# Block 1: another order of weight groups, its second item in f16 halves, and the weights' scales ahead of its first item

## The chip, the cores and the metric

The kernel runs on one core of one Trainium2 chip. The metric is device microseconds of one execution; lower is better. The time before is the median of three runs.

## What is computed

Linear attention with two softmaxes gives a matrix x of 4608 tokens by 512; a two-layer network with an unusual activation follows it.

```python
def _attn_ref(q, k, v):                       # each (8, 8, 576, 64), f32
    q_s = softmax(q, axis=-1)                 # written out: max, exp, sum + 1e-9
    k_s = softmax(k, axis=2)
    kv = np.einsum('bhsd,bhse->bhde', k_s, v)
    return np.einsum('bhsd,bhde->bhse', q_s, kv)

def _moe_ref(x, w_in, w_out):                 # (4608, 512), (512, 2048), (2048, 512)
    h = x @ w_in
    sp = np.maximum(h, 0.0) + np.log1p(np.exp(-np.abs(h)))
    g = h * erf(sp)
    return g @ w_out
```

w_in and w_out arrive as 64-bit floats, two 32-bit words to a number, and the kernel decodes them to f32 itself.

## The kernel before

**Items.** The tokens are cut into 4 pairs of batches, a pair (1152 tokens) into 3 blocks of 384, and the hidden width of 2048 into 4 groups of 512. One block with one group is an *item*; there are 48, numbered n in the order of `seq` (L942). Item n has a first product `m{n}` (x of the block by w_in of the group, in four parts m{n}.0 to m{n}.3), then on ScalarE softplus `T{n}` and erf `G{n}`, on VectorE the product with h `U{n}`, and a second product `M{n}` with w_out of the group, in three parts by 128 tokens, added up in PSUM over the block's four items. T and G each load a table on ScalarE.

**Two forms.** Items below `N32` = 6 run in f32: `mm1_32` (L1027) is 16 matmuls of 128x384, with four ScalarE copies out of PSUM, and `mm2` has 12 matmuls of 128x512. Items from 6 on run in f16 halves, high and low, of both operands with three products for one: `mm1` (L974) is seven block products in a scheme with fewer multiplications (84 matmuls of 128x192, evacuated by three ScalarE copies and four VectorE operations), and `mm2` has 36 matmuls of 128x512. For such an item VectorE also makes the high half `I{n}` (a cast, L1092) and the low half `O{n}` (a subtraction, L1096) of the activated values.

**What the f16 form needs.** Each weight half-matrix (a *job* j of `JOBS`: in 0, in 1, out 0, in 2, out 1, in 3, out 2, out 3) is loaded, decoded (`D`, VectorE) and squared for its maximum (`Q`, ScalarE). When all eight are squared, `Z` (`wscales`, L254) reduces the maxima, turns them on TensorE (8 transposes into the banks pY and pZ), and computes scales and the units U and V on VectorE. Then `S{j}` (`wsplit`, L306) writes the high halves on ScalarE and the low halves on VectorE (`split2`, L299 to L301) and, for a w_in, also four sums in place (L327); `R{j}` splits the sums. S{j} writes where the staged f32 of job j-2 lay. `f` (`finish`, L374) does the same for the block's x: an even f splits the parts as they are, an odd f the differences, in place in the f32 x that `mm1_32` of the block reads.

**Order.** `ORDER` (L33) is written out by hand up to item 5. Behind it a loop (L1225) emits, for n from N32 on, U{n-1}, the parts of m{n} with I{n-1}, O{n-1} and M{n-2} between them, then the splits that `SPLITS` (L46) names for n, then T{n} and G{n}. The attention of batches 1 to 7 is a generator: a token `A` in ORDER takes one step of it, and in the loop `pace` (L1208) takes steps as items go by. Batch 1 has 17 steps; the first step of a batch is the maximum over k on VectorE (L518 to L522), the second its transposes kT on TensorE with the reduction km (L529, L533) and the subtraction of q's maximum for the first four heads (L465, L466). ORDER takes 19 steps. Exponentials of a batch from 2 on, softplus and erf keep their written order on ScalarE.

The framework then schedules all engines' instructions, with the written order as priority: an instruction that is ready may run ahead of one that is not, so that the trace shows some steps earlier than the text has them. At run time each engine's own order is fixed.

Of the kernel before, what the change touches and what calls it, by code (L numbers as in the profile page):

```python
# [35 lines left out]
    m0.0 m0.1 D0.0.1 D0.1.1 D1.0 D1.1 m0.2 m0.3 T0 G0 Q0  # L36
    D2.0 A m1.0 D2.1 m1.1 U0 m1.2 m1.3 T1 G1 Q1 A A D3.0 M0.0 D3.1 M0.1 M0.2 Q2 U1 A A
    m2.0 D4.0 m2.1 D4.1 m2.2 m2.3 T2 G2 Q3 A A D5.0 M1.0 D5.1 M1.1 M1.2 U2 A A Q4 D6.0
    m3.0 D6.1 m3.1 D7.0 m3.2 D7.1 m3.3 T3 G3 A A A A A A A A A A Q5 U3 Q6 Q7
    M2.0 M2.1 M2.2 m4.0 m4.1 Z m4.2 m4.3 T4 G4 M3.0 f0 M3.1 M3.2 S0 R0 m5.0 m5.1 U4 m5.2 m5.3  # L40
    T5 G5 f1 S1 R1
"""


N32 = 6
SPLITS = {6: "S2 S4", 7: "S6 f2 f3 S3 R3", 8: "S5 R5", 9: "S7"}  # L46

SHARES = [2.51, 0, 0.16, 0.09, 1.58, 2.43, 1.12, 0.26, 0.29, 0.04, 0.78, 1.12, 0.16]
LEAD = 2.0
# [7 lines left out]
def attn_moe_kernel(  # L57
# [14 lines left out]
    NP = B // 2  # L72
# [6 lines left out]
    NG = NF // FG  # L79
# [3 lines left out]
    NBK = PT // T  # L83
# [260 lines left out]
    def act(out_, in_, func, chain=True, **kw):  # L344

        with ExitStack() as es:
            if chain and last[0] is not None:
                es.enter_context(tc.issue_after(last[0]))
            i = nc.scalar.activation(out_, in_, func, **kw)  # L349
        if chain:  # L350
            last[0] = i.ins
        return i
# [19 lines left out]
    x_next = [1]  # L372
# [555 lines left out]
    def out_dmas(p, tt, src):  # L928
# [11 lines left out]


    seq = [  # L942
        (p, bk, (g + 2 * (p == 0 and bk == 1)) % NG)
        for p in range(NP) for bk in range(NBK) for g in range(NG)
    ]
    N = len(seq)
# [96 lines left out]
    def unit(b, g):  # L1043

        U = bat[b]["U"][:, g:g + 1]
        if b < 2 and (b, g) not in udone:
            udone.add((b, g))
            nc.vector.tensor_tensor(U, w_u["in"][:, g:g + 1], bat[b]["ux"], op=ALU.mult)
        return U
# [3 lines left out]
    def flat(t):  # L1053
        return t.rearrange("p f t -> p (f t)")

    def in_chain(n):
        return CHAIN_FROM <= n < N - CHAIN_TAIL

    def softplus(n):
        s, g = st[n], seq[n][2]  # L1060
        s["G"] = ch.tile([P, FG, T], F32, tag="G", bufs=2, name=f"G_{n}")
        for o, w, b in spans(n):
            h, sp = s["H"], s["G"]
            h, sp = (flat(t) if w == T else t[:, :, o:o + w] for t in (h, sp))
            u = 1.0 if n < NG else bat[b]["ux"] if n < N32 else unit(b, g)
            act(sp, h, AF.Softplus, chain=in_chain(n), scale=u)
# [5 lines left out]
    def gmul(n):  # L1072
        s, g = st[n], seq[n][2]
        if n < NG:
# [3 lines left out]
        nc.vector.scalar_tensor_tensor(  # L1078
            flat(s["G"]), flat(s["G"]), GA32 if n < N32 else GA[:, g:g + 1], flat(s["H"]),
            op0=ALU.mult, op1=ALU.mult,  # L1080
        )
        if n < N32:
            return
# [18 lines left out]
    def mm2(n, tt):  # L1102
# [8 lines left out]
        ts_ = slice(tt * P, (tt + 1) * P)  # L1111
        if n < N32:
            w = stg[jn].rearrange("p (a e) -> p a e", a=FG)
# [37 lines left out]
    def tok(name):  # L1151

        if name != "A":
            if name in done:
                return
            done.add(name)
        if name in steps:
            dep, f = steps[name]
            assert all(x in emitted_steps for x in dep.split()), name
            f()  # L1160
            emitted_steps.add(name)
            if all(f"y{c}" in emitted_steps for c in range(NC4)):
                bat[0]["xdone"] = True
            return
        c = name[0]
        if c == "A":
            r = next(att, None)
            share[0] += r or 0
            return r
        x = [int(i) for i in name[1:].split(".")] if name[1:] else []  # L1170
        if c == "w":
            warm(*x)
        elif c == "D":
            with tc.issue_after(decoded[0].ins) if x[2:] == [1] else ExitStack():
                wdecode(NPC * x[0] + x[1], *x[2:])
        elif c == "Q":
            wsquares(*x)
        elif c == "S":
            wsplit(*x)
        elif c == "R":  # L1180
            wsplit_sums(*x)
        elif c == "f":
            xready(x_next[0])
            finish(x[0] % 2)
        elif c == "Z":
            wscales()
        elif c == "m":
            (mm1_32 if x[0] < N32 else mm1)(*x)
            emitted.add(("m", *x))
        elif c == "M":  # L1190
            mm2(*x)
            emitted.add(("M", *x))
        else:
            fn[c](*x)
# [13 lines left out]
    def pace(at_n):  # L1208


        at_n += LEAD
        k = NBK * NG + NG
        if at_n < k:
            goal = w_odd + (at_n - n1) * per_pair / (k - n1)
        else:
            goal = w_odd + per_pair + (at_n - k) * per_pair / (NBK * NG)
        while share[0] < goal:
            if not tok("A"):
                break
# [4 lines left out]
    FIN = 2  # L1224
    for n in range(N32, N + 2):  # L1225
        m0, m1, m2 = n < N, n - 1 < N, n - 2 < N
        if m1:
            tok(f"U{n - 1}")
        for i in range(4):
            if m0:  # L1230
                tok(f"m{n}.{i}")
            if N32 < n <= N and i < 2:
                tok(f"{'IO'[i]}{n - 1}")
            if m0 and n % NG == FIN and n > N32 and i < 2 and x_next[0] < NP * NBK:
                tok(f"f{fi[0]}")
                fi[0] += 1
            if m2 and i < 3:
                tok(f"M{n - 2}.{i}")
                pace(n + (i + 1) / NTT)
        for o in SPLITS.get(n, "").split():  # L1240
            tok(o)
        if m0:
            tok(f"T{n}")
            tok(f"G{n}")
# [32 lines left out]
```

## Time and profile before

| | |
|---|---|
| median of 3 runs | 839.77 us (837.84 to 843.3) |
| the profiled execution | 839.42 us, span 837.6 us |
| TensorE busy | 811.6 us, 97% |
| VectorE busy | 624.0 us, 74% |
| ScalarE busy | 503.9 us, 60% |

The span is the time from the first to the last instruction of the profiled execution; the device time lies 1.8 us above it. TensorE's matmuls are pipelined: the time of one is read from start to start of neighbours, and a row's duration is longer than that. In the timelines a group of like instructions is one row, with its count, and the idle time of the engine in front of it in brackets, with what ended it.

### The profile page before, as it was taken

How to read it: one execution, taken by the hardware profiler on the slowest of the kernel's cores; microseconds unless marked ns; L12 is line 12 of the kernel's file. 1: busy time of each engine (PE TensorE's matmuls, PEld its weight loads, DVE VectorE, ACT ScalarE, POOL GpSimd, SP SyncE). 2: the span in 40 equal slices, each digit the busy share in tenths (PEclk: the TensorE clock that was granted, in tenths of full speed). 3: DMA queues.
4: the chain of work that ended last, by engine and by line, in shares of the span. 5: the costliest groups of instructions: out<-in, count | busy, mean ns of one | idle time of the engine just before them, and what ended most of it. 6: DMA issues, size and time to landing. Idle time of an engine off the chain costs nothing.

```text
span 837.6 us, 15532 instructions
## 1 busy us (share of the span) xinstructions
PE 811.6 (97%) x6546; PEld 547.3 (65%) x6546; DVE 624.0 (74%) x887; ACT 503.9 (60%) x645; POOL 15.9 (2%) x37
## 2 busy tenths in 40 slices
PE   5999999999999999999999999999999999999996
PEld 4555455676666667767676676766776766767762
DVE  6999889998898779767875779857875657554543
ACT  2797759876665746645754556555764565544432
POOL 2101000000000000000000000000000000000000
PEclk9999999999999999999999999999999999999999
DMA  9995710041127205311362204411130100100100
GB/s 259 408 223 183 185 44 38 1 108 39 51 55 154 77 1 105 91 27 27 84 125 51 64 2 93 104 26 27 54 62 14 39 1 1 39 1 1 39 1 38
DMA packets 141348, 61.55 MB, mean 73 GB/s; under 512 B 130528, under 2 KB 132576, under 8 KB 141280
## 3 DMA queue, kind: packets, MB, share of 16 engines
q1 hardware_dynamic: 139104, 52.18, 25.1%
q0 software_dynamic: 2176, 8.39, 2.8%
q8 instruction: 51, 0.84, 0.4%
q14 instruction: 17, 0.14, 0.1%
HBM read 45.09 MB, written 9.44 MB: 65 GB/s over the span
## 4 chain that ended last, share of the span: by engine, by line
PE 59%; DVE 19%; ACT 13%; DMA 4%; issue 3%; SPq 2%; ACTq 0%; DVEq 0%
PE o L1124 25%; PE pX L998 14%; PE pZ L998 6%; ACT G L349 4%; ACT L349 4%; PE pY L998 3%; DVE G L1078 3%; DVE H L1096 2%; PE o L1115 2%; SPq L420 2%; DMA q<-in_q_dram 2%; PE pX L1037 2%; PE kv L565 1%; DVE x L301 1%; PE x L680 1%
## 5 line engine op out<-in xcount | busy, mean ns | idle before, releaser
L1124 PE MATMUL o<-wt,H 128*128 128x512 f16 x1512 | 347.3, 379 | 1.7 <-DVE H L1092 1.3
L998 PEld LDWEIGHTS <-wt 128*128 128x128 f16 x3528 | 293.1, 98 | 37.3 <-issue 15.8
L1124 PEld LDWEIGHTS <-H 128*128 128x128 f16 x1512 | 145.9, 98 | 150.9 <-DVE H L1092 1.8
L998 PE MATMUL pX<-x,wt 128*128 128x192 f16 x2016 | 194.3, 246 | 6.2 <-DVE H L1020 3.3
L349 ACT ACT_TABLE_LOAD x104 | 133.4, 1283 | 8.7 <-DVE H L1023 6.9
L1078 DVE SCALAR_TENSOR_TENSOR G<-G,small,H 128x1536 f32<-128x1536 f32 x44 | 80.0, 1818 | 55.3 <-ACT G L349 55.2
L1025 ACT COPY H<-pX 128x384 f32<-128x384 f32 x42 | 19.9, 474 | 139.2 <-PE pX L998 139.2
L998 PE MATMUL pZ<-x,wt 128*128 128x192 f16 x1008 | 98.4, 246 | 0.0
L349 ACT ACTIVATE G<-H,U 128x768 f32<-128x768 f32 (+1 forms) x56 | 69.2, 1253 | 22.1 <-DVE H L1023 21.5
L1096 DVE TENSOR_TENSOR H<-G,H 128x1536 f16<-128x1536 f32 x42 | 73.7, 1755 | 0.8
L349 ACT ACTIVATE G<-G 128x1536 f32<-128x1536 f32 x48 | 71.2, 1484 | 0.5
L998 PE MATMUL pY<-x,wt 128*128 128x192 f16 x504 | 48.4, 246 | 0.0
L454 ACT ACTIVATE x<-x 128x384 f32<-128x384 f32 (+1 forms) x52 | 16.2, 397 | 48.0 <-PE x L680 48.0
L1023 DVE TENSOR_TENSOR H<-pZ,H 128x384 f32<-128x384 f32 x42 | 23.2, 552 | 26.3 <-PE pZ L998 26.2
L1010 DVE COPY H<-pY 128x384 f32<-128x384 f32 x42 | 23.2, 553 | 26.1 <-PE pY L998 26.0
L300 ACT ACTIVATE x<-x 128x768 f16<-128x768 f32 (+1 forms) x44 | 33.0, 764 | 15.4 <-DVE x L393 15.4
L1092 DVE CAST H<-G 128x1536 f16<-128x1536 f32 x42 | 40.2, 957 | 0.8
L301 DVE SCALAR_TENSOR_TENSOR x<-x,x 128x768 f16<-128x768 f32 (+1 forms) x44 | 37.3, 851 | 3.2 <-ACT x L300 3.2
L1140 DVE TENSOR_SCALAR ob<-o,V 128x512 f32<-128x512 f32 x29 | 21.7, 747 | 21.1 <-PE o L1124 21.1
L1037 PE MATMUL pX<-x,wt 128*128 128x384 f32 x96 | 34.0, 488 | 0.0
L1012 DVE TENSOR_TENSOR H<-pX,H 128x384 f32<-128x384 f32 x42 | 23.3, 555 | 13.7 <-PE pX L998 12.9
L465 DVE TENSOR_REDUCE q_m<-q 128x16 f32<-128x1024 f32 x14 | 17.0, 1216 | 18.0 <-DMA q<-in_q_dram 18.0
(183 smaller groups left out, 818.8 us busy)
## 6 DMA issues: line engine op xcount, KB each, us to landing
out_dram<-ob SPq DMA_DIRECT2D x32, 256.0 KB, 2.3
vbuf<-in_v_dram SPq DMA_DIRECT2D x56, 128.0 KB, 3.2
q<-in_q_dram SPq DMA_DIRECT2D x56, 128.0 KB, 3.2
k<-in_k_dram SPq DMA_DIRECT2D x56, 128.0 KB, 3.2
wt<-in_moe_w_out_dram POOLq DMA_DIRECT2D x5, 1024.0 KB, 6.5
wt<-in_moe_w_in_dram SPq DMA_DIRECT2D x4, 1024.0 KB, 12.0
wt<-in_moe_w_out_dram SPq DMA_DIRECT2D x2, 1024.0 KB, 15.7
H_raw<-in_k_dram SPq DMA_DIRECT2D x2, 512.0 KB, 4.6
```

The lines of the kernel that those rows point to most:

```text
L300: nc.scalar.activation(hi, src, AF.Copy, scale=s)
L301: nc.vector.scalar_tensor_tensor(lo, src, s, hi, op0=ALU.mult, op1=ALU.subtract)
L349: i = nc.scalar.activation(out_, in_, func, **kw)
L998: nc.tensor.matmul(o, w[wl][:, c, a * P:(a + 1) * P], x[:, xl, xi, c, :], start=(new and a == 0 and c == 0 and i == 0), stop=(c == 1 and i ...
L1010: nc.vector.tensor_copy(C[0, 0], bank2("Y"))
L1012: add(C[0, 0], bank2("X"), C[0, 0], op=ALU.add)
L1023: add(C[0, 1], bank2("Z"), C[0, 1], op=ALU.add)
L1037: nc.tensor.matmul(ph[:, :T], w[:, c, a * P:(a + 1) * P], x[:, c, :], start=(c == 0), stop=(c == NC4 - 1),)
L1078: nc.vector.scalar_tensor_tensor(flat(s["G"]), flat(s["G"]), GA32 if n < N32 else GA[:, g:g + 1], flat(s["H"]), op0=ALU.mult, op1=ALU.mult,)
L1092: nc.vector.tensor_copy(flat(s["gh"]), flat(s["G"]))
L1096: nc.vector.tensor_tensor(flat(s["gl"]), flat(s["G"]), flat(s["gh"]), op=ALU.subtract)
L1124: nc.tensor.matmul(o, s[gt][:, a, ts_], w[wl][:, a, :], start=(first_ and a == 0 and i == 0), stop=(last_ and a == FG - 1 and i == 2),)
```

## The change

Three things. Block 1's four items take the groups in the order 3 0 1 2 instead of 2 3 0 1, so that item 4 has group 3 and items 5, 6, 7 have groups 0, 1, 2. `N32` becomes 5: item 5, the second of block 1, runs in f16 halves. And in the order written by hand Z stands in front of m4, two attention steps fewer are taken (17, which is batch 1; the other two, the first of batch 2, are left to `pace`), f1 comes directly behind S0 and R0, and the splits from S1 on move into the loop, where they follow one another in the order in which items 6 to 11 need them. The last edit keeps the loop's own `f` steps where they were (from n = 10 on), now that N32 is smaller.

```diff
-    m3.0 D6.1 m3.1 D7.0 m3.2 D7.1 m3.3 T3 G3 A A A A A A A A A A Q5 U3 Q6 Q7
-    M2.0 M2.1 M2.2 m4.0 m4.1 Z m4.2 m4.3 T4 G4 M3.0 f0 M3.1 M3.2 S0 R0 m5.0 m5.1 U4 m5.2 m5.3
-    T5 G5 f1 S1 R1
+    m3.0 D6.1 m3.1 D7.0 m3.2 D7.1 m3.3 T3 G3 A A A A A A A A Q5 U3 Q6 Q7
+    M2.0 M2.1 M2.2 Z m4.0 m4.1 m4.2 m4.3 T4 G4 M3.0 f0 M3.1 M3.2 S0 R0 f1
 """
 
 
-N32 = 6
-SPLITS = {6: "S2 S4", 7: "S6 f2 f3 S3 R3", 8: "S5 R5", 9: "S7"}
+N32 = 5
+SPLITS = {4: "", 5: "S1 R1 S2", 6: "S3 R3 S4", 7: "S6 f2 f3", 8: "S5 R5", 9: "S7"}
@@
     seq = [
-        (p, bk, (g + 2 * (p == 0 and bk == 1)) % NG)
+        (p, bk, (g + 3 * (p == 0 and bk == 1)) % NG)
         for p in range(NP) for bk in range(NBK) for g in range(NG)
     ]
@@
-            if m0 and n % NG == FIN and n > N32 and i < 2 and x_next[0] < NP * NBK:
+            if m0 and n % NG == FIN and n > 2 * NG and i < 2 and x_next[0] < NP * NBK:
                 tok(f"f{fi[0]}")
                 fi[0] += 1
```

## Rows read from the trace of the kernel before

**Rows 1.** The page: busy time of each engine, then tenths in 40 slices.

```profile
PE 811.6 (97%) x6546; PEld 547.3 (65%) x6546; DVE 624.0 (74%) x887; ACT 503.9 (60%) x645; POOL 15.9 (2%) x37
...
PE   5999999999999999999999999999999999999996
...
DVE  6999889998898779767875779857875657554543
```

**Rows 2.** Busy time by stretch: us, engines' busy us (count), clock, DMA.

```profile
110.14:217.60 107.46, 104.37 (x683) 66.52 (x682) 98.17 (x157) 77.14 (x95) 0.63 (x2) 1.00 0.19 49
217.60:837.60 620.00, 607.76 (x5343) 424.91 (x5341) 429.90 (x594) 351.03 (x414) 2.52 (x8) 1.00 0.20 47
```

**Rows 3.** TensorE's timeline, m4 to m9: start us, us, line, out<-in, count, [idle before].

```profile
110.14 2.74 PE L1037 MATMUL pX<-x,wt 128*128 128x384 f32 x8
113.50 0.63 PE L529 MATMUL kT<-ident,asc 128*128 128x128 f32 x4 [0.62 <-DVE asc L522]
...
116.55 0.60 PE L264 MATMUL ws_out<-ident,small 128*128 128x128 f32 x4
...
122.59 10.46 PE L1115 MATMUL o<-rw,G 128*128 128x512 f32 x24
132.89 2.74 PE L1037 MATMUL pX<-x,wt 128*128 128x384 f32 x8
...
143.21 1.15 PE L998 MATMUL pY<-x,wt 128*128 128x192 f16 x12
...
149.35 1.07 PE L998 MATMUL pX<-x,wt 128*128 128x192 f16 x11 [0.45 <-DVE x L301]
...
182.61 1.15 PE L998 MATMUL pY<-x,wt 128*128 128x192 f16 x12
...
184.59 2.75 PE L1124 MATMUL o<-wt,H 128*128 128x512 f16 x12
187.18 0.27 PE L125 MATMUL x_bk<-ident,mx 128*128 128x128 f32 x1
...
198.37 1.15 PE L998 MATMUL pX<-x,wt 128*128 128x192 f16 x12 [0.91 <-DVE H L1020]
```

**Rows 4.** Groups by line over the span: busy us, mean ns | idle before.

```profile
L998 PEld LDWEIGHTS <-wt 128*128 128x128 f16 x3528 | 293.1, 98 | 37.3 <-issue 15.8
```

**Rows 5.** VectorE's timeline, from the maxima's reduction to f3's last piece.

```profile
108.63 0.18 DVE L258 TENSOR_REDUCE small<-sq 128x8 f32<-128x32 f32 x1
...
113.28 1.20 DVE L465 TENSOR_REDUCE q_m<-q 128x16 f32<-128x1024 f32 x1
...
118.27 0.69 DVE L268 TENSOR_REDUCE wse_in<-ws_in 128x4 f32<-128x512 f32 x1 [2.06 <-PE ws_in L264]
...
122.04 3.14 DVE L301 SCALAR_TENSOR_TENSOR wt<-wt,small,wt 128x1024 f16<-128x1024 f32 x3
...
126.36 3.69 DVE L327 TENSOR_TENSOR wt<-wt 128x512 f32<-128x512 f32 x6
...
132.48 4.87 DVE L301 SCALAR_TENSOR_TENSOR wt<-wt,small,wt 128x1024 f16<-128x1024 f32 x4
...
165.43 1.27 DVE L301 SCALAR_TENSOR_TENSOR wt<-wt,small,wt 128x1024 f16<-128x1024 f32 x1
...
176.78 0.95 DVE L1092 CAST H<-G 128x1536 f16<-128x1536 f32 x1
177.65 0.55 DVE L1020 TENSOR_TENSOR H<-pX,H 128x384 f32<-128x384 f32 x1
178.11 1.75 DVE L1096 TENSOR_TENSOR H<-G,H 128x1536 f16<-128x1536 f32 x1
179.78 0.95 DVE L301 SCALAR_TENSOR_TENSOR x<-x,x 128x768 f16<-128x768 f32 x1
```

**Rows 6.** ScalarE's timeline: T4 from its table load, G4's erf.

```profile
124.39 1.28 ACT L349 ACT_TABLE_LOAD   x1
...
129.22 1.48 ACT L349 ACTIVATE G<-G 128x1536 f32<-128x1536 f32 x1
```

## Prediction

> **What bounds the kernel now.** I read the busy line and the slices first [rows 1]: TensorE is busy 811.6 of 837.6 us, and after the first of the 40 slices it falls below nine tenths only in the last. VectorE is at 74% over the span, but unevenly: its digits are 8 and 9 in the first third and 5 to 7 later. So I cut the span at the end of item 2's second product (110.14) and at the end of item 9's first part (217.60), the stretch that the change touches [rows 2]. The granted clock is 1.00 in both parts. In the first TensorE is busy 104.37 of 107.46 us, VectorE 98.17, ScalarE 77.14. From 217.60 to the end VectorE is busy 429.90 of 620.00. The reader is to see two things: a microsecond of TensorE work that goes away shortens the program if nothing makes TensorE wait in its place, and in just this stretch VectorE has only 9 us left over.
>
> The profiled execution took 839.42 us (span 837.6), which is 0.35 below the median of 839.77. All sums are made against 839.42. About 1%, 8.4 us, is what a measurement of this kernel can tell from no change.
>
> **The change part by part.**
>
> *Item 5 on TensorE.* In f32 its first product is four tiles, from 132.89 to 143.21: 10.32 us. An f32 second product runs from 122.59 to 132.89: 10.30 us [rows 3]. In f16 halves the first product is seven groups of 12 matmuls, two of which took 1.98 (182.61 to 184.59), so 6.93 us; the second is three groups of 2.59 (184.59 to 187.18), so 7.77 us. Item 5 therefore gives back 3.39 + 2.53 = 5.92 us of TensorE. The new order of groups (item 4 is group 3, items 5, 6, 7 are groups 0, 1, 2) costs nothing by itself: same shapes, same count.
>
> Against that stands a rule. The f16 halves need 120 weight loads for item 5 where f32 needs 56 records. A load of f16 weights has a mean of 98 ns [rows 4], and yet the pitch of the 192-column matmuls is 0.99/12 = 82 ns [rows 3]: less than one load, so loads must run under matmuls and under each other. The Trainium skill, "TensorE: Matmul & The Clock Gate", Part 3 (The mechanism), says that a weight load overlaps with matmuls in flight only where the row group differs; here all 128 rows are used each time, so by that rule every load would stand in series. This trace contradicts it, so I keep 14.70 us for the f16 item.
>
> *Scales (Z) in front of m4.* Today the transposes start inside m4, at 116.55 [rows 3], although the maxima they turn were there from the reduction at 108.63 [rows 5]. VectorE idles 2.06 us for the second set of them, and the first split starts at 122.04: 5.49 us after 116.55. In front of m4 they run at 110.14, so splits can start at 110.14 + 5.49 = 115.6, which is 6.4 earlier. The transposes are the same eight, so TensorE pays nothing more; m4 waits for nothing of Z but for the bank of m4.1, which is read within 2 us while m4.0 runs 2.58. Should the reduction be late, nothing covers TensorE: it has 1.3 us to spare (110.14 against 108.63 and its 0.2).
>
> *The two steps of batch 2's attention later.* The k maximum, its transposes (kT) and the first q subtraction lose their early place. TensorE waited 0.62 us in front of kT at 113.50 [rows 3]; that wait goes, kT itself moves behind M4. On VectorE, the second q subtraction and km, which ran from 113.28 to 116.21 (2.06 before 118.27) [rows 5], no longer fit in front of Z's answers: 2.93 us go behind them. The first q subtraction and the k maximum can still run in the gap around 107 to 113, since instructions that are ready run ahead of their place here: S5 of item 8's turn ran at 165.43 [rows 5]. No DMA is moved by these two steps, on SP or POOL; loads of batch 3 hang on later steps.
>
> *Item 5 on VectorE and ScalarE.* VectorE gains the cast (0.87, 176.78 to 177.65), the low half (1.67, 178.11 to 179.78) and four evacuations of 0.47 each (177.65 to 178.11), 4.4 us in all [rows 5]. ScalarE loses one of four copies, at nothing.
>
> *The splits earlier.* All of them still run, none twice. What changes is when they are due. S0, R0 and f1 are due at m5 instead of m6, and f1 must wait for m4 to have read the block, until the eight transposes (some 0.9, the four of kT took no more than 0.63) and m4's 10.3 have run from 110.14 on, so to 121.4. M3 covers TensorE from there to 131.7. VectorE needs for S0 4.3 us (low halves of 1.22 and 0.62, four sums of 0.61), for R0 two of 1.22 and for f1 3.6 (four subtractions of the size of an evacuation, 0.47, two halves of 0.87), 10.3 in all [rows 5]: from 115.6 to 125.9. So m5 does not wait by this sum, with 5.8 us to spare. After that S1, R1, S2, S3, R3 follow one item ahead of their old place.
>
> *Where it gets tight.* I follow VectorE to the last piece of f3, which m8.1 needs. Today it ends at 179.78 + 0.87 = 180.65 [rows 5], and m8 starts at 182.61 [rows 3]. After the change: 180.65 + 4.4 (item 5) + 2.9 (moved behind Z) - 6.4 (Z earlier) - 2.5 (S5's two low halves and one sum, 1.22, 0.62 and 0.61, which ran early as filling and are not due) = 179.1. TensorE would reach m8 at 182.61 - 5.92 - 0.62 = 176.1, or at 175.6 if the short wait on the way (0.45 at 149.35 [rows 3]) vanishes as well. So VectorE, which was 2 us ahead of TensorE at this point, will be behind it: by 3.5 at most, or by 1.5 if m8.0, which runs 1.98 and needs only f2, goes first. M6 could cover it altogether if its halves are ready. The bounds are 0 and 3.5 here, and again up to 0.9 at m9, where TensorE already waits for VectorE (198.37 [rows 3]). I take 2.0 for both together, nearer to the wait of 0.45 at 149.35, where M4 filled in, than to a full stop.
>
> *Sum:* -5.92 - 0.62 + 2.0 = -4.5 us, all of it in hand by about 217; behind that TensorE's work is the same and VectorE is at 69%. 839.42 - 4.5 = 834.9 us.
>
> **The rivals.**
>
> 1. *Nothing gets short.* M6 covers f3, and the waits at 149.35 and 198.37 vanish: -5.92 - 0.62 - 0.45 - 0.91 = -7.9, so 831.5. For it: M4 covered the late f1 at 149.35 but for 0.45. Against it: M5 is 2.53 shorter as a cover, and ScalarE's k and q exponentials stand in front of item 6's softplus.
>
> 2. *VectorE sets the pace through item 9.* Everything that it does up to 199 stays due; then TensorE is where VectorE lets it be: today's wait at 198.37, plus 4.4 + 2.9 - 6.4 = +0.9. The gain is gone but for what it wins back later: 837 to 840. For it: 98.17 busy of 107.46 [rows 2]. Against it: S5, R5 and S7, about 9 us, are not due until m11 and M11.
>
> 3. *Slower: m5 waits at its head.* Place: the high halves of f1 on ScalarE. T4 and G4 are issued ahead of them, and took from 124.39 to 130.70 today [rows 6]. If, in addition, VectorE takes S1 and R1 (6.7) first, f1 ends not at 125.9 but at 125.9 + 6.7 + 6.3 = 138.9, and m5.1, due at 133.7, waits 5.2; M4 cannot fill in, as it needs U4, which stands behind G4. It decides from a wait of 4.5 us on (5.92 + 0.62 less the 2.0 at m8 and m9); at 5.2 the time is 840.1, and if U4 and the copies of M3's output get in front too, some 4 us more, 844. Against it: f1's subtractions can run from 121.4, ahead of T4's end.
>
> 4. *Loads in series.* This is a mechanism by rows: if each of item 5's 120 f16 matmuls paid its load of 98 ns on top of its pitch, the item would cost 14.70 + 11.8 = 26.5 us instead of 20.6, and the program 839.42 + 5.9 - 0.6 = 844.7. The pitch of 82 ns excludes it. (This is the rule of the Trainium skill named above, "TensorE: Matmul & The Clock Gate", Part 3.)
>
> **How the numbers follow.** Forecast (a gain of 2.5 to 6, so 833.4 to 837): 0.56. Rival 1 (830.5 to 833.4): 0.21. Rival 2 (837 to 840.5): 0.14. Rival 3 (839.9 to 850): 0.08. Rival 4: 0.01. Predicted is 834.9. The range leaves out the lower edge of rival 1 (0.06) and most of rival 3 (0.06 with rival 4): 831.0 to 841.0. Faster by over 1% means below 831.4, which is more than all the TensorE work and the waits counted: only the edge of rival 1, 0.08. Slower by over 1% means over 848.2: the far part of rival 3, several such delays behind one another, 0.03. Within 1%: 0.89.
>
> **What would show it right or wrong.** In the changed profile: m5 in f16 shapes starts right behind M3, near 131.7, with no wait over 1 us (rival 3 falls, or shows here). The ws transposes stand ahead of m4 near 110 and the first split of weights starts on VectorE near 115.6. TensorE's records fall by one item's f32 groups, its busy time by 5.9. Item 8's first matmul starts between 175 and 179; a wait there names VectorE's x halves (L301) if my tight place is right, ScalarE's copies if the exponentials are. Item 10, at 217.60 today, starts 4 to 6 earlier, and from there the two traces run side by side. I am wrong if a wait of over 3 us appears on TensorE between 110 and 217, or if that lead is lost later.

## The result, and the profile after

The changed kernel took 831.78 us (median of 5 runs, 831.66 to 833.22), 0.9916 of the kernel before [0.9895, 0.9936]: 7.1 us less by the ratio (the medians lie 8.0 apart; the ratio is used throughout). The forecast of 834.9 was 3.1 too high. The time lies inside the stated range, but in the bracket of rival 1 (830.5 to 833.4), not in that of the forecast (833.4 to 837). The same kernel run once more gave 0.9917 [0.9898, 0.9936].

The profiled execution took 833.08 us, of which 831.2 are the span. The page of the changed kernel, its busy line (the line numbers here are smaller by one than those of before, so L997 is L998 there):

```profile
PE 804.8 (97%) x6610; PEld 546.8 (66%) x6610; DVE 626.6 (75%) x894; ACT 503.4 (61%) x644; POOL 15.9 (2%) x37
```

TensorE's busy time fell by 6.8 us [rows 1], VectorE's rose by 2.6. To see where the time went I cut both kernels in three: from the end of M2 to item 10's first matmul (the stretch of [rows 2]; it begins with the transposes of Z now), from there to item 16's (the middle), and the rest. Busy time by stretch of the changed kernel (us, then each engine's busy us with its count, clock, DMA):

```profile
110.91:212.89 101.98, 98.91 (x747) 66.63 (x746) 100.78 (x164) 76.71 (x94) 0.63 (x2) 1.00 0.20 51
212.89:312.58 99.69, 97.36 (x931) 68.96 (x930) 83.34 (x122) 63.87 (x77) 0.63 (x2) 1.00 0.29 64
312.58:831.20 518.62, 509.96 (x4415) 355.90 (x4412) 346.59 (x474) 287.13 (x337) 1.89 (x6) 1.00 0.18 45
```

Before, the same view gives 100.97 us for the middle (217.60 to 318.57, clock 1.00) and 519.03 for the rest, which two are one row of [rows 2]. The stretch went from 107.46 [rows 2] to 101.98, so 5.48 less, of which 5.46 is TensorE's busy time (104.37 to 98.91); in it VectorE is now busy 100.78 of 101.98 us. The middle is 1.28 shorter and the rest 0.41: 7.17 in all. The head before the stretch was 0.77 longer (110.91 against 110.14) in this execution, of which 0.46 stand in front of TensorE's first transposes (9.11 us against 8.65); so the spans differ by 6.4 only. In the kernels below with Z in front of m4 this head takes 109.7 to 111.6, and 115.5 in one.

TensorE's timeline of the changed kernel, to be held against [rows 3] (start us, us, line, out<-in, count, [idle before]):

```profile
110.91 0.60 PE L263 MATMUL ws_in<-ident,small 128*128 128x128 f32 x4
...
132.40 1.15 PE L997 MATMUL pY<-x,wt 128*128 128x192 f16 x12
133.39 1.15 PE L997 MATMUL pX<-x,wt 128*128 128x192 f16 x12
134.38 1.35 PE L997 MATMUL pZ<-x,wt 128*128 128x192 f16 x12
136.00 1.15 PE L997 MATMUL pY<-x,wt 128*128 128x192 f16 x12 [0.27 <-DVE H L1009]
137.67 1.16 PE L997 MATMUL pX<-x,wt 128*128 128x192 f16 x12 [0.51 <-DVE H L1011]
...
178.24 1.15 PE L997 MATMUL pY<-x,wt 128*128 128x192 f16 x12
...
180.22 2.75 PE L1123 MATMUL o<-wt,H 128*128 128x512 f16 x12
182.92 1.15 PE L997 MATMUL pZ<-x,wt 128*128 128x192 f16 x12
...
193.93 1.15 PE L997 MATMUL pY<-x,wt 128*128 128x192 f16 x12
...
203.14 0.66 PE L661 MATMUL qT<-ident,q 128*128 128x128 f32 x4 [1.41 <-ACT x L453]
```

The reader is to see that m5 (132.40) is in f16 and starts right behind M3, that m8 (178.24) does not wait although VectorE is full (m8.0 runs until M6 starts at 180.22; m8.1, which needs the end of f3, stands behind that at 182.92), and that small waits have moved to other places: 0.27 and 0.51 in m5 and m6, 1.41 in front of qT.

### The profile page after: what moved, and what is told of

The parts are those of the page before. It is cut to its first block, busy times and chain, and to the rows that moved or that the text cites. A ratio compares the mean times of both kernels' runs of the same rounds, so it can differ in the third digit from the quotient of the medians.

```text
span 831.2 us, 15665 instructions
## 1 busy us (share of the span) xinstructions
PE 804.8 (97%) x6610; PEld 546.8 (66%) x6610; DVE 626.6 (75%) x894; ACT 503.4 (61%) x644; POOL 15.9 (2%) x37
## 4 chain that ended last, share of the span: by engine, by line
PE 55%; DVE 27%; ACT 9%; issue 3%; DMA 3%; SPq 3%; POOL 0%; ACTq 0%; DVEq 0%; POOLq 0%
PE o L1123 27%; PE pX L997 13%; PE pZ L997 7%; DVE G L1077 3%; PE pY L997 3%; ACT G L348 3%; ACT L348 3%; DVE H L1095 3%; DVE wt L300 2%; SPq L419 2%; DVE x L300 2%; DMA q<-in_q_dram 2%; DVE H L1091 2%; DVE x L392 1%; PE x L679 1%
## 5 line engine op out<-in xcount | busy, mean ns | idle before, releaser
L1123 PE MATMUL o<-wt,H 128*128 128x512 f16 x1548 | 356.0, 379 | 1.7 <-DVE H L1091 1.3
L997 PEld LDWEIGHTS <-wt 128*128 128x128 f16 x3612 | 300.0, 98 | 36.5 <-issue 14.3
L1123 PEld LDWEIGHTS <-H 128*128 128x128 f16 x1548 | 149.2, 98 | 154.0 <-DVE H L1091 1.8
L997 PE MATMUL pX<-x,wt 128*128 128x192 f16 x2064 | 198.8, 246 | 3.8 <-DVE H L1019 2.4
L1077 DVE SCALAR_TENSOR_TENSOR G<-G,small,H 128x1536 f32<-128x1536 f32 x44 | 79.9, 1817 | 53.3 <-ACT G L348 53.0
L997 PE MATMUL pZ<-x,wt 128*128 128x192 f16 x1032 | 100.6, 246 | 0.0
L348 ACT ACTIVATE G<-H,U 128x768 f32<-128x768 f32 (+1 forms) x58 | 71.0, 1241 | 22.1 <-DVE H L1022 21.5
L1095 DVE TENSOR_TENSOR H<-G,H 128x1536 f16<-128x1536 f32 x43 | 75.5, 1755 | 0.8
L997 PE MATMUL pY<-x,wt 128*128 128x192 f16 x516 | 49.6, 246 | 0.3 <-DVE H L1009 0.3
L1009 DVE COPY H<-pY 128x384 f32<-128x384 f32 x43 | 23.8, 553 | 25.7 <-PE pY L997 25.7
L299 ACT ACTIVATE x<-x 128x768 f16<-128x768 f32 (+1 forms) x44 | 32.9, 765 | 15.2 <-DVE x L392 15.1
L1011 DVE TENSOR_TENSOR H<-pX,H 128x384 f32<-128x384 f32 x43 | 23.9, 555 | 13.2 <-PE pX L997 12.4
L1036 PE MATMUL pX<-x,wt 128*128 128x384 f32 x80 | 28.3, 488 | 0.2 <-DVE wt L219 0.2
```

The source lines that it names most:

```text
L299: nc.scalar.activation(hi, src, AF.Copy, scale=s)
L997: nc.tensor.matmul(o, w[wl][:, c, a * P:(a + 1) * P], x[:, xl, xi, c, :], start=(new and a == 0 and c == 0 and i == 0), stop=(c == 1 and i ...
L1009: nc.vector.tensor_copy(C[0, 0], bank2("Y"))
L1011: add(C[0, 0], bank2("X"), C[0, 0], op=ALU.add)
L1036: nc.tensor.matmul(ph[:, :T], w[:, c, a * P:(a + 1) * P], x[:, c, :], start=(c == 0), stop=(c == NC4 - 1),)
L1077: nc.vector.scalar_tensor_tensor(flat(s["G"]), flat(s["G"]), GA32 if n < N32 else GA[:, g:g + 1], flat(s["H"]), op0=ALU.mult, op1=ALU.mult,)
```

## The experiments

The first question was which of the parts brings the gain: TensorE's lighter item, or the edits of order. The second, whether VectorE, busy nearly all the stretch, sets a price there. The third, whether one more step of the same kind would pay. Gains in us are the ratio's distance from that of the changed kernel, times 838.

**Two edits of order without the f16 item.** The kernel before, with Z in front of m4 and two attention steps fewer:

```diff
-... T3 G3 A A A A A A A A A A Q5 ...
-    M2.0 M2.1 M2.2 m4.0 m4.1 Z m4.2 m4.3 ...
+... T3 G3 A A A A A A A A Q5 ...
+    M2.0 M2.1 M2.2 Z m4.0 m4.1 m4.2 m4.3 ...
```

> The kernel before, with only the scales put in front of m4 and two attention steps fewer in the written order; item 5 stays in f32 and the groups stay 2 3 0 1. Theory A (the gain is item 5's 5.92 us of TensorE work, the order only lets it be had): 0 to 1.0 us faster than before, the wait of 0.62 at kT; ratio 0.998 to 1.000. Theory B (a good part comes from the waits that the earlier scales and the later steps take away, here and later on): 2 us faster or more, ratio 0.9975 or less.

It took 839.11 us, 1.0008 [0.9988, 1.0027]. Its stretch:

```profile
111.16:218.07 106.91, 104.86 (x682) 66.60 (x681) 97.39 (x156) 77.70 (x95) 0.63 (x2) 1.00 0.19 49
```

The stretch is 0.55 shorter than before and the middle 0.85 (100.12), but the head is 1.02 longer: it has a wait of 1.2 us in front of a qT there, where before had none. So by themselves these two edits of order give nothing that can be measured. (The order of groups, the place of f1 and that of the later splits were not taken alone beside the f32 item.) Against this kernel the changed one has 5.95 us less TensorE work in the stretch (104.86 to 98.91) and 1.02 more idle time (2.05 to 3.07, what the span leaves over the busy time).

**The f16 item without one of the edits of order.**

```diff
-    M2.0 M2.1 M2.2 Z m4.0 m4.1 m4.2 m4.3 ...
+    M2.0 M2.1 M2.2 m4.0 m4.1 Z m4.2 m4.3 ...
```

> The changed kernel with the scales back between m4.1 and m4.2; all else changed. Theory A with its sum by VectorE: the splits start at about 121.5 instead of 116.6, f1's last piece, which came at 135.4 and held TensorE by about 0.6, comes some 2 to 5 us later, and TensorE waits that much more at m5: 2 to 5 us slower than the changed kernel, 834 to 837. Theory B: over 5 us of the gain go. Rival C (the scales' place doesn't matter, other work fills in): within 1 us of the changed kernel.

It took 835.66 us, 0.9970 [0.9954, 0.9986]: about 4.4 us of the gain are lost. In its profile the stretch is 1.45 longer than in the changed kernel (103.43) and the middle 1.44 (101.13). Z's transposes run 4.1 us later than in the changed kernel (111.34), and TensorE waits for halves of x and of weights:

```profile
115.40 0.60 PE L263 MATMUL ws_out<-ident,small 128*128 128x128 f32 x4
...
135.30 1.07 PE L997 MATMUL pZ<-x,wt 128*128 128x192 f16 x11 [0.45 <-DVE x L300]
...
164.38 1.00 PE L997 MATMUL pZ<-x,wt 128*128 128x192 f16 x10 [0.77 <-DVE wt L300]
```

So the edit that was worth nothing beside the f32 item is worth about 4 us beside the f16 item. The two profiles account for 2.9 of it. VectorE's busy time shows how: in the stretch it is 98.22 us in place of 100.78, and in the middle 86.04 in place of 83.34. Z in its old place holds up some 2.6 us of VectorE's work until behind item 10; that the rest of the 4 us comes the same way is not shown.

**The two attention steps back in their early place.**

```diff
-... T3 G3 A A A A A A A A Q5 ...
+... T3 G3 A A A A A A A A A A Q5 ...
```

> The changed kernel with the two attention steps of batch 2 back in their early place. Theory A: the k maximum ran early in the changed kernel anyhow, as filling (110.58 to 116.68), so what comes back is the wait at kT (0.6) and a little VectorE work in front of the splits: 0 to 1.5 us slower. Theory B: 2 us slower or more.

832.89 us, 0.9920 [0.9885, 0.9956]: the same as the changed kernel, and so is the stretch (102.05). This part does not matter within that interval: the k maximum starts just ahead of M2's end in both (at 110.58 in the changed kernel), although the changed text leaves that step to `pace`.

**The old order of groups under the f16 item.** Item 5 is group 3 then. A job may be split only when the one two places ahead of it in `JOBS` is, so group 3's first half-matrix (job 5) needs jobs 1 and 3 split ahead of it, three splits in place of one:

```diff
-        (p, bk, (g + 3 * (p == 0 and bk == 1)) % NG)
+        (p, bk, (g + 2 * (p == 0 and bk == 1)) % NG)
-... M3.0 f0 M3.1 M3.2 S0 R0 f1
+... M3.0 f0 M3.1 M3.2 S1 R1 S3 R3 S5 R5 f1
-SPLITS = {4: "", 5: "S1 R1 S2", 6: "S3 R3 S4", 7: "S6 f2 f3", 8: "S5 R5", 9: "S7"}
+SPLITS = {4: "", 5: "S0 R0 S7", 6: "S2 S4", 7: "S6 f2 f3"}
```

> The changed kernel with block 1's groups in the old order 2 3 0 1, so that item 5 has group 3: its weights are split only behind groups 1 and 2 of w_in (S1 R1 S3 R3 S5 R5 in front of m5 instead of S0 R0), since each split writes where the one two jobs before was staged. By the VectorE sum two more S and R, 13.4 us, stand in front of m5, against 131.7 to 133.7 as its due time and 135.4 as the time at which f1 ended: m5 waits 8 to 13 us, and the kernel is 2 to 7 us slower than the changed one by what the later splits then save. If VectorE isn't what item 5 waits for, within 1 us of the changed kernel.

845.88 us, 1.0082 [1.0053, 1.0112]: about 14 us more than the changed kernel. TensorE's timeline, and two windows of 6 us from 140 on:

```profile
146.80 0.69 PE L543 MATMUL kB<-ident,km 128*128 128x128 f32 x2 [4.45 <-DVE km L532]
...
150.26 1.78 PE L997 MATMUL pY<-x,wt 128*128 128x192 f16 x10 [1.57 <-DVE wt L300]
```

```profile
140.00:146.00 6.00, 2.35 (x9) 1.07 (x7) 5.94 (x7) 4.67 (x4) 0.00 (x0) 0.93 0.00 0
146.00:152.00 6.00, 3.63 (x20) 2.71 (x21) 6.00 (x7) 3.77 (x3) 0.00 (x0) 0.50 0.00 0
```

VectorE is full throughout, and km, a reduction of 0.7 us, stands behind the splits on it. This is the one half of rival 3, splits on VectorE in front of m5, though m5 waits for its weights here (150.26) and not for f1. It was larger than I expected: over the wait the granted clock fell (0.93 in the first window, 0.50, the 1.2 GHz level, in the second), and ten matmuls took 1.57 us (150.26 to 151.83) where twelve take 0.99. The order of groups costs nothing on TensorE, as the prediction says; what it decides is how many splits stand in front of item 5.

**More VectorE work, early and late.** The low half of two items is computed twice, in one kernel at items 5 and 6, and in another kernel, as the control, at items 29 and 30 (the condition reads `n in (29, 30)` there): about 3.3 us of VectorE each time.

```diff
         nc.vector.tensor_tensor(flat(s["gl"]), flat(s["G"]), flat(s["gh"]), op=ALU.subtract)
+        if n in (5, 6):
+            nc.vector.tensor_tensor(flat(s["gl"]), flat(s["G"]), flat(s["gh"]), op=ALU.subtract)
```

> The changed kernel with the low half of items 5 and 6 (O5, O6, 1.67 us each) computed twice, so 3.3 us more for VectorE between 155 and 180, where it is busy 49.8 of 50 us. If VectorE sets the pace in the tight stretch (the forecast's term of 2.0, rival 2), the kernel gets 2.5 to 3.5 us slower. If the splits S5, R5 and S7, 9 us that are not due until items 11 and M11, give way (rival 1), 0 to 1 us slower.

> The same 3.3 us of VectorE work put at items 29 and 30, where VectorE is busy some 7 of 10 us: a control. By both theories 0 to 0.7 us slower than the changed kernel; the difference between the two kernels is what the tight stretch charges.

Early: 835.81 us, 0.9970 [0.9950, 0.9990]. Late: 832.15 us, 0.9935 [0.9917, 0.9954]. The early work costs 2.9 us against the control and 4.4 against the changed kernel, so about all of its duration. The late work costs 1.6 by the ratio, which the two intervals do not tell from nothing. The early price falls due late in the stretch and, for the larger part, behind it. Busy time by stretch with the early work (to item 10, then to item 16), and TensorE's timeline:

```profile
110.05:213.26 103.21, 99.53 (x746) 66.65 (x745) 102.14 (x162) 76.66 (x94) 0.63 (x2) 1.00 0.19 48
213.26:314.81 101.55, 97.49 (x932) 68.99 (x930) 84.92 (x126) 63.73 (x77) 0.63 (x2) 1.00 0.29 64
```

```profile
249.71 1.15 PE L997 MATMUL pY<-x,wt 128*128 128x192 f16 x12
```

This row is m12, 139.66 us behind M2's end (110.05); in the changed kernel this is 136.45. So 3.2 us are spent by then: 1.2 in the stretch (103.21 against 101.98) and 2.0 between items 10 and 12.

**Less VectorE work.** The low halves of items 5 and 6 are left out (the high ones stand in for them), which takes the same 3.3 us away.

```diff
+        if n in (5, 6):
+            s["gl"] = s["gh"]
+            return
         nc.vector.tensor_tensor(flat(s["gl"]), flat(s["G"]), flat(s["gh"]), op=ALU.subtract)
```

> The changed kernel without the low halves of items 5 and 6: O5 and O6 are left out and the second product takes the high half in their place, so TensorE does the same work and VectorE 3.3 us less in the tight stretch. This leaves out a part of the computation. The counterpart of more_vector_early, which cost 3 us and more. If VectorE still holds TensorE up in the changed kernel by what the forecast put at 2.0 us, 1 to 2 us faster than the changed kernel. If the two are just level there, so that more VectorE work costs and less gains nothing, 0 to 0.7 us faster.

832.70 us, 0.9938 [0.9922, 0.9955]: no gain, and the stretch is 102.29. Together the two say that TensorE and VectorE are level from item 5's low half on (156.57 in the changed kernel): VectorE work that is added there is paid in full, VectorE work that is taken away gives nothing. TensorE is busy 99.21 of the 102.29 us then, and its longest wait, 1.0 at qT, is for ScalarE. The waits in m5 and m6 (134 to 138) lie ahead of the work taken away, so this test says nothing of them.

**f1 ahead of item 4's softplus and erf.** It is to tell whether the small waits in m5 and m6 come from ScalarE's order (T4 and G4 in front of f1's high halves, as rival 3 has it).

```diff
-... m4.3 T4 G4 M3.0 f0 M3.1 M3.2 S0 R0 f1
+... m4.3 f0 S0 R0 f1 T4 G4 M3.0 M3.1 M3.2
```

> The changed kernel with f0 S0 R0 f1 written ahead of T4 G4 M3 instead of behind them. If the waits at m5 and m6 (0.6 hidden in a group of matmuls at 134.38, then 0.27 and 0.51) come from f1's high halves behind T4 and G4 on ScalarE, as rival 3 had it, f1 ends near 128 instead of 135.4, these waits go, and the kernel is 0.5 to 1.5 us faster than the changed one, unless U4, 3 us later by it, holds M4. If they come from VectorE's queue alone, no change.

831.73 us, 0.9923 [0.9907, 0.9939]: no change. TensorE's rows at m5 and m6, VectorE's, and ScalarE's G4 with f1's second high half:

```profile
134.88 1.15 PE L997 MATMUL pY<-x,wt 128*128 128x192 f16 x12 [0.55 <-DVE H L1009]
136.54 1.15 PE L997 MATMUL pX<-x,wt 128*128 128x192 f16 x12 [0.51 <-DVE H L1011]
```

```profile
131.68 0.95 DVE L300 SCALAR_TENSOR_TENSOR x<-x,x 128x768 f16<-128x768 f32 x1
132.55 1.81 DVE L1077 SCALAR_TENSOR_TENSOR G<-G,small,H 128x1536 f32<-128x1536 f32 x1
134.28 0.55 DVE L1009 COPY H<-pY 128x384 f32<-128x384 f32 x1
```

```profile
128.97 1.49 ACT L348 ACTIVATE G<-G 128x1536 f32<-128x1536 f32 x1
130.36 0.83 ACT L299 ACTIVATE x<-x 128x768 f16<-128x768 f32 x1
```

f1 ends at 132.55 here. M2 ends 1.2 us earlier too (109.70 against 110.91), so of the 2.9 us to the changed kernel 1.6 are f1's own. The wait is the same: U4 (L1077) now stands between f1 and the copy that frees the bank, so these waits are for VectorE's queue. ScalarE's order is tested by half only: the schedule put the first high half ahead of G4 (at 125.51), and left the second behind it, where it was.

**The next step of the same kind: item 4 in f16 too.** Groups 0 1 2 3, N32 = 4, and the splits one item earlier:

```diff
-    M2.0 M2.1 M2.2 Z m4.0 m4.1 m4.2 m4.3 T4 G4 M3.0 f0 M3.1 M3.2 S0 R0 f1
+    M2.0 M2.1 M2.2 Z f0 M3.0 M3.1 M3.2 S0 R0 f1
-N32 = 5
-SPLITS = {4: "", 5: "S1 R1 S2", 6: "S3 R3 S4", 7: "S6 f2 f3", 8: "S5 R5", 9: "S7"}
+N32 = 4
+SPLITS = {4: "S1 R1 S2", 5: "S3 R3 S4", 6: "S5 R5 S6", 7: "f2 f3 S7"}
```

> One step further: item 4 in f16 halves as well (N32 = 4, groups 0 1 2 3, Z f0 M3 S0 R0 f1 behind M2, splits one item earlier still). If TensorE's work decides: 5.9 us less, 826. If VectorE and ScalarE decide: only M3 stands between the scales and m4, and all eight splits, 40 us of VectorE with f1, are due within m4 to M7; VectorE gets 4.4 us more and the due splits S5, R5 and S7 can no longer give way, so TensorE waits 6 to 15 us between m4 and m8 and the kernel is 0 to 9 us slower than the changed one, 832 to 841. I hold the second for likelier.

838.84 us, 1.0007 [0.9997, 1.0016]: about 7.5 us slower than the changed kernel, though a second item is lighter by the same 5.9. The window from 130 to 150, and two rows of TensorE:

```profile
130.00:150.00 20.00, 14.10 (x137) 11.27 (x135) 20.00 (x26) 19.69 (x21) 0.00 (x0) 1.00 0.01 1
```

```profile
134.07 1.15 PE L997 MATMUL pX<-x,wt 128*128 128x192 f16 x12 [1.58 <-DVE H L1019]
...
139.44 0.49 PE L997 MATMUL pZ<-x,wt 128*128 128x192 f16 x4 [1.46 <-ACT H L1014]
```

VectorE is busy all of the 20 us and ScalarE 19.69; TensorE only 14.10. What was level is now VectorE's and ScalarE's, which is rival 2 one step further on.

**The weights' sums on GpSimd.** GpSimd is idle in the stretch, so the 16 sums of the splits, 10.7 us on VectorE, were moved there, in the changed kernel and in the one with item 4:

```diff
-            nc.vector.tensor_tensor(A[o], A[x], A[y], op=op)
+            nc.gpsimd.tensor_tensor(A[o], A[x], A[y], op=op)
```

> The changed kernel with the four in-place sums of each w_in split on GpSimd instead of VectorE: 16 operations of 128x512, 0.61 us each on VectorE, so 9.8 us off VectorE between 116 and 190; on GpSimd one of that size took 1.03 to 1.05 us in the start-up. Theory D (VectorE's queue is what TensorE waits for in the stretch, and 3.3 us more of it cost 3.3): the unmarked and marked waits at m5, m6 and up to m12 shrink, 0.5 to 2 us faster than the changed kernel; no more, since TensorE is at 98% there. Rival E (GpSimd's operations hold VectorE's up, or the sums come later by their longer chain, 4.2 us for four): VectorE's operations beside them get longer than the 0.61, 1.22 and 1.67 us of pitch read so far, and the kernel is not faster, or up to 3 us slower. The Trainium skill, GPSIMD Engine Reference, Key specifications, has the SBUF interfaces shared with VectorE, with contention where VectorE reads two SBUF inputs, as its split operations do; that would speak for E.

> Item 4 in f16 halves as well (as in item4_too), with the 16 sums on GpSimd. In item4_too TensorE was busy 14.1 of 20 us from 130 to 150 while VectorE was busy 20.0 of 20. By theory D 9.8 us less on VectorE give back 5 to 9 us of the 13 that item4_too lost against its TensorE work: 830 to 834. By rival E nothing comes back: 837 to 841.

848.19 us, 1.0110 [1.0082, 1.0139], and 853.18 us, 1.0160 [1.0132, 1.0188]: 13 to 16 us worse than without the move. Groups by line of the first, from 110 to 200 (busy us, mean ns of one, then idle before), and the sums' durations (ns, min/median/max):

```profile
L326 POOL TENSOR_TENSOR wt<-wt 128x512 f32<-128x512 f32 x16 | 27.7, 1736 | 63.1 <-DVE wt L300 40.5 <-issue 21.6
```

```profile
L326 POOL TENSOR_TENSOR wt<-wt x16: 1262/1372/3317, 117.6 to 182.9; 128x512 f32<-128x512 f32 x16
```

and of the changed kernel, in its second run:

```profile
L326 DVE TENSOR_TENSOR wt<-wt 128x512 f32<-128x512 f32 x16 | 10.7, 682 | 0.0
```

A sum takes 1.74 us on average in place of 0.68, and the sums of a split hang on each other; ScalarE's and TensorE's steps behind them come late. T4's table load starts at 134.02 (123.16 in the changed kernel), and f1's high halves stand behind T4 and G4, at 140.71. TensorE's timeline and two windows:

```profile
141.61 0.32 PE L997 MATMUL pZ<-x,wt 128*128 128x192 f16 x1 [7.98 <-ACT x L299]
```

```profile
138.00:146.00 8.00, 3.20 (x20) 2.76 (x20) 5.71 (x6) 7.99 (x9) 0.00 (x0) 0.50 0.23 90
146.00:152.00 6.00, 5.55 (x47) 4.17 (x46) 6.00 (x7) 3.05 (x4) 2.94 (x1) 0.99 0.03 12
```

TensorE waits 7.98 us at one place, for the first of f1's high halves (ACT x L299): the place and the cause that rival 3 names. The granted clock is at 0.50 in the window in which that wait ends.

**The changed kernel once more**, for the size of the gain.

> The changed kernel itself once more, on the chip of the next two kernels, for a narrower ratio to the kernel before. From the first measurement 0.9916; if that is right, 0.990 to 0.9935 again. A ratio nearer to 0.9945 would be my forecast of 4.5 us.

832.53 us, 0.9917 [0.9898, 0.9936], the stretch 101.68, the middle 99.20, the rest 518.3.

## Why the prediction was nearly right, step by step

*Item 5 on TensorE, -5.92: held.* Beside the kernel with the two edits of order alone TensorE's busy time in the stretch fell by 5.95. Beside the kernel before it fell by 5.46: these two differ by 0.49 with the same f32 work, so the size is known to about half a microsecond. The rival by which every weight load stands in series is out: the groups of m5 at 132.40 and 133.39 are 0.99 apart, as in [rows 3].

*The wait in front of kT, -0.62: held in the stretch.* It is gone from both kernels with Z in front of m4; the stretch of the one with the f32 item is 0.55 shorter.

*Z in front of m4.* The first split was to start at 115.6. It started at 116.60; of that one microsecond 0.77 is the later head. VectorE's timeline of the changed kernel, to be held against [rows 5], and ScalarE's, to be held against [rows 6]:

```profile
116.60 3.13 DVE L300 SCALAR_TENSOR_TENSOR wt<-wt,small,wt 128x1024 f16<-128x1024 f32 x3
...
128.34 1.21 DVE L464 TENSOR_REDUCE q_m<-q 128x16 f32<-128x1024 f32 x1
129.60 1.22 DVE L465 TENSOR_TENSOR q<-q,q_m 128x1024 f32<-128x1024 f32 x1
130.74 1.81 DVE L1077 SCALAR_TENSOR_TENSOR G<-G,small,H 128x1536 f32<-128x1536 f32 x1
132.47 1.28 DVE L300 SCALAR_TENSOR_TENSOR wt<-wt,small,wt 128x1024 f16<-128x1024 f32 x1
133.66 1.82 DVE L300 SCALAR_TENSOR_TENSOR x<-x,x 128x768 f16<-128x768 f32 x2
135.40 0.55 DVE L1009 COPY H<-pY 128x384 f32<-128x384 f32 x1
...
178.29 0.95 DVE L300 SCALAR_TENSOR_TENSOR x<-x,x 128x768 f16<-128x768 f32 x1
```

```profile
128.00 1.48 ACT L348 ACTIVATE G<-G 128x1536 f32<-128x1536 f32 x1
...
130.89 1.57 ACT L299 ACTIVATE x<-x 128x768 f16<-128x768 f32 x2
```

*"So m5 does not wait": wrong in its reason, nearly right in its price.* I had f1 end at 125.9; it ended at 135.40. Its subtractions were done by 127.6. Its high halves came on ScalarE only at 130.89 to 132.46, behind T4 and G4 (128.00), and a low half is the difference to its high half, so VectorE could not make it sooner. Then the low halves stood behind U4 (130.74) and a split (132.47) on VectorE, which had filled the time with q's step (128.34 and 129.60). The first delay is the cause that rival 3 names; I had set it aside because the subtractions can run early, which they did. The second is VectorE's queue: what is ready there runs in the gaps that a written order leaves, and I had applied that only to steps of attention. How the 9.5 us divide between the two was not tested apart. It cost little, because m5's first two groups need nothing of f1, the third only the earlier half, and m6's groups were put in between: 1.62 us from 134.38 to 136.00 where a group takes 0.99, and the wait of 0.51 at 137.67. That is 1.14 in all, and the two marked waits in it are for copies that free a bank (L1009, L1011), late on VectorE behind f1 and a split.

*The tight place at m8: the place right, the price not.* f3's last piece was to end at 179.1; it ended at 178.29 + 0.87 = 179.16. m8 was to start at 176.1, or between 175 and 179; it started at 178.24, later than 176.1 by the head's 0.77, by the 1.14 at m5 and m6, and 0.2 more. So VectorE was 0.9 behind TensorE there and not 3.0 to 3.5, and m8.0, which runs until 180.22, covers that by itself; M6, on which rival 1 counted, was not needed. There is no wait in front of m9 (193.93) either. VectorE's busy time in the stretch rose by 2.6 where item 5 was put at 4.4; its rows rose by 7, so no work is missing, and the rest was not followed. The term of 2.0 that I set for new waits at m8 and m9 is the one that was mis-sized: at those two places it is 0. Idle time of TensorE in the stretch is 3.09 before [rows 2] (107.46 less 104.37) and 3.07 after, so the waits that went (0.62 at kT, 0.45 and 0.91 [rows 3], 0.42 for a copy) were replaced by as much elsewhere, 0.27 and 0.51 at m5 and m6, 0.83 at kv, 1.41 at qT where before had 0.7. Predicted was 1.4 more idle (2.0 less 0.62). TensorE's waits in the stretch (sum, times, longest), of before the one at qT:

```profile
PE qT L662 <- ACT x L454: 0.7, 1, 0.7
```

and of the changed kernel the one at kv, the only one above 0.2 that is not in the timeline above:

```profile
PE kv L564 <- ACT k L348: 0.6, 1, 0.6
```

None of the changed kernel's is a wait of m8 or m9 for VectorE; that of qT, a step of attention between two parts of m9, is for ScalarE.

*"Behind that TensorE's work is the same": so it is, but 1.7 us were gained there.* The middle is 1.28 shorter and the rest 0.41. In the middle one pair of rows differs. Before, VectorE waits 2.94 us for a load of q, and TensorE 2.09 some 9 us later:

```profile
291.20 1.22 DVE L465 TENSOR_REDUCE q_m<-q 128x16 f32<-128x1024 f32 x1 [2.94 <-DMA q<-in_q_dram]
...
300.33 1.15 PE L998 MATMUL pX<-x,wt 128*128 128x192 f16 x12 [2.09 <-DVE H L1020]
```

After, both are about 0.9 shorter:

```profile
285.21 1.22 DVE L464 TENSOR_REDUCE q_m<-q 128x16 f32<-128x1024 f32 x1 [2.04 <-DMA q<-in_q_dram]
...
294.34 1.15 PE L997 MATMUL pX<-x,wt 128*128 128x192 f16 x12 [1.20 <-DVE H L1019]
```

This accounts for 0.9 of the 1.28 if the one wait is the other's cause, which is argued from the rows and not shown: no run changed that load. Over all kernels the middle takes 98.98 to 101.55, without any tie to TensorE's work in the stretch (100.12 in the one with the work of before, 99.05 with the old groups, which came 14 us late). VectorE work that is held up into it lengthens it: the two longest are the one with more early VectorE work (101.55, VectorE busy 84.92) and the one with Z in its old place (101.13, 86.04). That does not explain the kernel before, whose VectorE is busy 83.28 in the middle, as in the changed one (83.34). What decides there is left open.

So of the 7.2 us that the three parts got shorter, the stretch gave 5.48 where 4.5 was forecast, and 1.7 came from where nothing was. Rival 1, at 0.21, was right that nothing gets short at m8 and m9, but for another reason, and too large for the stretch (7.9), where the 5.48 lies nearer to the forecast. That the whole gain comes so near to rival 1's is luck: the middle and the rest, which no part of the sum had, make up the difference.

## What to carry to other kernels

When one engine is the bound and another is nearly full, cutting work from the first pays only as far as the second has room: here the f16 item without the earlier scales gained 2.5 us, two of the edits of order without the f16 item nothing, and all together 7. Look for each lighter step at what it adds to the engine that is next in line, and for an edit that lets that engine start earlier. A late operand is not yet a wait: ask what else the engine has ready to fill the gap, and do the same for the engine that makes the operand.

## What the runs showed of the hardware

GpSimd's sum of two 128x512 f32 tiles takes from 1.26 to 3.32 us, 1.74 on average; VectorE does it in 0.68. While VectorE was idle or at a reduction, which reads one tile, it took 1.27 to 1.28 (the sums at 120.55, 121.90 and 153.81); the longest, 3.32 at 149.06, ran beside VectorE's splits, which read two. Either of the two can be the one held up: at 178.05 a sum took 1.28 and the subtraction beside it on VectorE 1.45.

VectorE itself suffered. Of its eight 128x384 subtractions three ran beside sums of GpSimd's and took 1.45 to 1.62 us, the other five 0.55. Two of them, the first beside sums that ran until 132.82:

```profile
131.62 1.62 DVE L392 TENSOR_TENSOR x<-x 128x384 f32<-128x384 f32 x1
...
135.24 0.55 DVE L392 TENSOR_TENSOR x<-x 128x384 f32<-128x384 f32 x1
```

The Trainium skill, "GPSIMD Engine Reference", section 1 (Specifications), says that GpSimd shares its SBUF interfaces with VectorE and contends with VectorE instructions of two SBUF inputs; the traces agree. Section 4.1 (Engine selection) of that page of the Trainium skill has GpSimd at about twice VectorE's time; undisturbed it is 1.9 times here (1.27 to 0.68), and 2.6 times by the mean, with the contention in it.

Waits of TensorE of 1.58 and 1.46 us left the granted clock at 1.00 (item 4 in f16, window above), and so did the 2.09 in the middle of the kernel before. Around the single waits of 4.45 and 7.98 us it fell to 0.50, and it was back at 0.99 in the window from 146 to 152 of the second; so a long wait there costs more than its length.
